# One transfer fills two exponential buffers, two are filled ahead, and the planner's thresholds are other ones

## The chip, the cores and the metric

The kernel runs on one core of a Trainium2 chip. The metric is the device time of one execution in microseconds (us). Five engines work side by side, each through its own list of instructions in a fixed order: PE multiplies matrices, ACT evaluates functions, DVE does element-wise work, POOL does small element-wise work and issues the transfers named here, and SP issues the other transfers. They wait for each other through semaphores. An engine that waits holds up everything behind it in its list.

## The reference

Four layers in a row, each added to its input: softmax attention (A), linear attention (B), then A and B again, with the same weights. There are 2048 rows of 512, 32 heads of 16; in A all heads share one key and one value.

```python
def _A_ref(x, wq, wk, wv, wo):
    q = (x @ wq).reshape(B, S, H, Dh).transpose(0, 2, 1, 3)
    k = x @ wk
    v = x @ wv
    scores = jnp.einsum("bhqd,bkd->bhqk", q, k) * (Dh ** -0.5)
    p = _softmax(scores, axis=-1)
    o = jnp.einsum("bhqk,bkd->bhqd", p, v)
    return o.transpose(0, 2, 1, 3).reshape(B, S, H * Dh) @ wo

def _B_ref(x, wqkv, wo):
    phi = lambda t: jnp.where(t > 0, t + 1, jnp.exp(t)) + 1e-6
    pq, pk = phi(q), phi(k)
    kv = jnp.einsum("bhsd,bhse->bhde", pk, v)
    num = jnp.einsum("bhqd,bhde->bhqe", pq, kv)
    den = jnp.einsum("bhqd,bhd->bhq", pq, z)[..., None] + 1e-6
    return (num / den) @ wo

x = A_x
x = x + _A_ref(_layernorm(x), ...)
x = x + _B_ref(_layernorm(x), ...)
x = x + _A_ref(_layernorm(x), ...)
x = x + _B_ref(_layernorm(x), ...)
```

## The kernel before

Nearly all the work is the exponential of the scores of the two A layers (layers 0 and 2): 2048 blocks of 128 keys x 512 (query, head) columns in each. PE makes a block of scores (L990, "QK") into a PSUM bank. Then it goes one of two ways.

- **ACT's way.** ACT takes the blocks of a set of two or three banks with one ACTIVATE with Exp (L1170), and PE multiplies the result with V (L1044, "PV").
- **DVE's way.** DVE turns a block into the int16 whose bits are a bf16 near the exponential (L1256, one TENSOR_SCALAR of 128x512). It collects four such blocks in one exponential buffer FB, a *chunk* of 128x2048. That approximation is bettered by averaging four copies whose int16 are shifted by 0, 32, 64 and 96, each with its own weight (VW, PV at L1044). So a chunk needs three shifted copies. DVE makes a shifted copy with one TENSOR_SCALAR of 128x2048 (L1304). One of the three can be made by transfers instead: POOL issues a *fill* that writes the constant row `shift_row`, which lies in DRAM, into every partition of a free FB buffer (L1328, in `prime`), and later a *shift*, a transfer that adds the chunk to the filled buffer (L1337, in `dma_shift`). Such a chunk costs DVE two shifts and not three.

FB has 12 buffers of its own. Up to five more are lent to it from tensors that lie idle (OBB, sacc, xn, wq, wo2), which is why the profile names those as outputs of L1256, L1304, L1328 and L1337 too. PT, OBB and xnT hold ACT's results in the same way.

The order on every engine is set when the program is built. `Planner` plays the program through with a duration for each operation and starts on each engine the operation with the best priority that is ready. What it started in which order is what the engines run. Which way a block goes, and when a buffer is filled, is decided there by thresholds: `BLS`, `BLT`, `BLO` and `DXB` (how much may be queued on DVE), `FBO`, `FBS` and `FBP` (how many FB buffers must stay free), `CHT`, `CHE` and `ENDL` (how near the end of the work DVE stops taking blocks), `NPRE` (how many buffers are filled ahead), `DMIN`, `DQ` and `AHEAD` (when a chunk's shift goes to a transfer), `LAG`, `STICK` and `SWITCH` (order of operations that are nearly ready). `DPF`, `DXF` and `DTAIL` are the planner's durations for transfers. The table `TUNE` changes thresholds when an A layer starts. It changes globals, so that what table 0 sets stays in force in layer 2 unless table 2 sets it again.

Layer by layer: **stream 1** is layer 0, in which the B layer's first tiles run between the blocks as x rows come out. After it comes **the transition**, in which layer 1 ends and the K and Q of layer 2 are made. `act_stream` of layer 2 starts with the first two K tiles; DVE takes blocks from the time when all 16 K tiles are made (`KGATE`), and from there on is **stream 2**. **The tail** is the end of layer 3.

Of the kernel before, what the change touches and what calls it, by code (L numbers as in the profile page):

```python
# [8 lines left out]
I16 = mybir.dt.int16  # L9
# [3 lines left out]
PE, AC, DV, PO, SP = "pe", "act", "dve", "pool", "sp"  # L13
ENGS = (PE, AC, DV, PO, SP)

P = 128
# [19 lines left out]
class Planner:  # L36
# [43 lines left out]
    def op(self, opts, reads=(), writes=(), prio=5.0, lat=0.08, dma=False, name="", join=None, mode="full", port=False, after=(), behind=(), xfer=None, trn=False):  # L80

        o = Op()
        o.opts, o.prio, o.users, o.done, o.end = opts, prio, [], False, None
        o.eng, o.fn, o.n, o.value, o.sem, o.signal, o.isdma = None, None, None, None, None, False, dma
        o.name = (name, lat)
        o.freed = False
        o.begun = None
        o.cols = 0
        o.mode = mode
        o.port = port  # L90
        o.xfer = xfer
        o.trn = trn
        deps = set()
        for k in reads:
            deps.update(self.ws(k))
        for k in list(writes) + list(after) + list(behind):
            deps.update(self.ws(k))
            deps.update(self.readers.get(k, ()))
        if join is not None:
            deps.update(join.deps)  # L100
            deps.discard(join)
        for k in writes:
            if join is not None and join in self.ws(k):
                self.writer[k] = self.ws(k) + [o]
            else:
                self.writer[k] = [o]
                self.readers[k] = []
        for k in list(reads) + list(after):
            if k not in writes:
                self.readers.setdefault(k, []).append(o)  # L110
        o.deps = deps
        o.left = 0
        chain = len(opts) == 1 and PE in opts
        for d in deps:
            if not (d.done or (chain and d.freed and d.eng == PE)):
                o.left += 1
                d.users.append(o)
        if o.left == 0:
            self._eligible(o)
        return o  # L120
# [235 lines left out]
class Seg:  # L356
# [11 lines left out]
    def take(self, js, back=False):  # L368
# [15 lines left out]
SWITCH = 0.107  # L384
# [6 lines left out]
LAG = 0.15  # L391
# [17 lines left out]
BLS = 1.4  # L409
BLO = 5.0  # L410
DXB = 2.0
BLT = 2.5
# [12 lines left out]
ENDL = 12  # L425
# [6 lines left out]
CHB = 4  # L432
FBO = 2
FBS = 4
AHEAD = 20
CHT = 19
PSH = False
STICK = 0.8
# [4 lines left out]
DMIN = 4  # L443
NPRE = 2
EVEN = True
CHE = 8
AVOID = True
PGEN = 0.95
DPF = 1.7
DXF = 3.2  # L450
DTAIL = 2.0
DQ = 4.0
FBP = 4
TUNE = {0: {"CHE": 2, "AHEAD": 10, "BLS": 1.7, "FBP": 2, "NPRE": 1, "DMIN": 3, "LAG": 0.1, "STICK": 2.0, "FBO": 1, "FBS": 4, "BLO": 7.0, "DXB": 0.8, "BLT": 3.2},
        2: {"CHE": 6, "CHT": 16, "FBS": 2, "AHEAD": 15, "BLO": 3.5, "DXB": 2.5, "FBP": 3, "DMIN": 2, "STICK": 0.8, "LAG": 0.1, "DQ": 5.0}}


def bass_interleave_layers__grouped_kv_mqa__linear_attn_block__prompt_kernel(
# [11 lines left out]
    pl = Planner(nc)  # L470
    op = pl.op
# [38 lines left out]
    NFB = 12  # L510
    FB = sb("FB", [P, NFB, CHB * 512], BF16)
# [58 lines left out]
    def guest(L, kind, i, h=None):  # L570
        return once((L, kind, i, h), home[kind, i]) if (kind, i) in home else ()
# [45 lines left out]
    fb_pool = Pool_(range(NFB))  # L617
# [92 lines left out]
    cst = nc.dram_tensor("shift_row", (1, CHB * 512), I16, kind="Internal").ap()  # L710

    def fb_keys(i):
        return [("FB", i, h) for h in range(CHB)]
# [56 lines left out]
    def until(*keys):  # L770
        for k in keys:
            yield ("ops", pl.ws(k))
# [55 lines left out]
    two = set()  # L828
# [152 lines left out]
    def run_a(L):  # L981
# [23 lines left out]
        def spend(h, o):  # L1005
            h[0] -= 1
            if o not in h[1]:
                h[1].append(o)
            if h[0] == 0:
                pl.give_after(h[2], h[3], h[1])  # L1010
# [85 lines left out]
        def act_stream():  # L1096
            if L == 0:
                globals().update(TUNE[0])
            yield ("flag", ("K", L, 0))
            globals().update(TUNE[L])  # L1100
            if L:
# [212 lines left out]
        primed = []  # L1314

        def prime():
            yield ("flag", ("K", L, T - 1))
            if L == 0:
                row = FB[0:1, NFB - 1, :].bitcast(I16)
                op({DV: (0.6, lambda e: e.memset(row, DSH * 128 // NSH))}, writes=fb_keys(NFB - 1), prio=1.0)  # L1320
                op({SP: (0.54, lambda e: e.dma_start(cst, row))}, reads=fb_keys(NFB - 1), writes=["cst"], prio=1.0, lat=2.5, dma=True)
            yield from until("cst")
            while state["si"] < len(segs) - DMIN:
                if len(primed) >= NPRE or len(fb_pool.free) <= FBP or fb_pool.wait:
                    yield ("sleep", 0.2)
                    continue
                g_ = yield ("acq", fb_pool, 9.0)
                o = op({PO: (PGEN, lambda e, g_=g_: e.dma_start(fbs[g_].bitcast(I16), cst.to_broadcast([P, CHB * 512])))}, reads=["cst"], writes=fb_keys(g_), prio=9.0,  # L1328
                       lat=0.3, dma=True, behind=guest(L, "FB", g_), xfer=(DPF, DTAIL))
                primed.append((g_, o))  # L1330
            while primed:
                g_, o = primed.pop()
                pl.give_after(fb_pool, g_, [o])

        def dma_shift(blk, f_, hold, g_, o):
            pl.stat["dma"] += 1
            o = op({PO: (PGEN, lambda e: e.dma_start(fbs[g_].bitcast(I16), fbs[f_].bitcast(I16), accum_op=ALU.add))}, reads=fb_keys(f_), writes=fb_keys(g_), prio=0.0, lat=0.3,  # L1337
                   dma=True, xfer=(DXF, DTAIL))
            spend(hold, o)
# [32 lines left out]

        pl.process(spare())
        pl.process(prime())
        for i in pairs:
            pl.process(spare_sacc(i))
# [564 lines left out]
```

## Time and profile before

| | |
|---|---|
| device time, median of 3 | 1484.33 us (1484.32 to 1484.44) |
| the profiled execution: its time, its span | 1484.35 us, 1482.5 us |
| granted TensorE clock | 1.00 |
| busy in the span: PE, DVE, ACT, POOL | 95%, 95%, 97%, 29% |
| fills (L1328) | 218 transfers of 512 KB |
| shifts by transfer (L1337) | 216 transfers of 512 KB |
| share of the 16 DMA engines taken by POOL's queue | 65.9% of the span |

The span runs from the first instruction to the last; the time has 1.85 us more, around the program. In a profile's rows "DVE FB L1256" is the DVE instruction of line 1256 that writes FB; xN is a number of instructions; "<-" names what ended the wait. An instruction's duration reaches about 0.08 to 0.2 us into the next one's, since the engines start the next before the last has drained. What an instruction costs an engine that is full is therefore the distance from its start to the next one's start, and "busy" counts such an engine as 100% even where short waits are hidden in the overlap.

### The profile page before, as it was taken

What the parts mean: (1) busy time and instruction counts of PE and PEld (TensorE: products, weight loads), DVE (VectorE), ACT (ScalarE), POOL (GpSimd) and SP (SyncE); (2) the same over time, 40 slices, a digit from 0 to 9 for tenths busy, and PEclk for the clock granted to TensorE, in tenths of its full rate; (3) what the DMA queues carried; (4) which work ended last, traced back from release to release, by engine and by line L of the source; (5) the groups of instructions that cost most, each with busy time, mean ns of one, the idle gap of its engine ahead of it and who ended that gap; (6) DMA issues with size and microseconds to landing.
All of it is one profiled execution on the core that took longest, in us unless ns stands there. A gap on an engine that the chain in (4) does not pass through costs nothing.

```text
span 1482.5 us, 40513 instructions
## 1 busy us (share of the span) xinstructions
PE 1415.0 (95%) x16387; PEld 512.6 (35%) x16387; DVE 1412.3 (95%) x2628; ACT 1441.2 (97%) x1536; POOL 424.9 (29%) x627
## 2 busy tenths in 40 slices
PE   7999999999999999999999999999999999999998
PEld 4433333333332323233644323333333333333235
DVE  7999999999999999998866899999999999999996
ACT  8999999999999999999799999999999999999996
POOL 5323333333333332300111223333323333223201
PEclk9999999999999999999999999999999999999999
DMA  4887898897888987710000458898879899879701
GB/s 116 229 205 194 185 212 188 203 215 179 195 204 197 217 192 168 187 43 2 2 2 2 104 136 200 201 211 205 212 188 226 201 211 215 203 183 216 172 1 58
DMA packets 76745, 240.14 MB, mean 162 GB/s; under 512 B 14993, under 2 KB 20113, under 8 KB 76562
## 3 DMA queue, kind: packets, MB, share of 16 engines
q0 software_dynamic: 62928, 229.14, 65.9%
q1 hardware_dynamic: 13634, 8.43, 2.0%
q8 instruction: 131, 2.15, 0.6%
q14 instruction: 52, 0.43, 0.1%
HBM read 120.62 MB, written 2.10 MB: 83 GB/s over the span
## 4 chain that ended last, share of the span: by engine, by line
PE 38%; DVE 35%; ACT 19%; issue 7%; POOL 1%; DMA 0%; ACTq 0%; DVEq 0%; POOLq 0%
PE ps L1044 15%; DVE FB L1256 14%; ACT PT L1170 12%; PE ps L990 12%; DVE FB L1304 7%; ACT xnT L1170 3%; PE ps L761 3%; PE ps L923 2%; PE ps L1089 2%; ACT OBB L1170 2%; PE ps L1410 2%; DVE wq L1256 1%; DVE xn L1256 1%; DVE sacc L1390 1%; PE ps L757 1%
## 5 line engine op out<-in xcount | busy, mean ns | idle before, releaser
L1170 ACT ACTIVATE PT<-ps 128x1024 bf16<-128x1024 f32 (+1 forms) x957 | 1004.8, 1163 | 5.4 <-PE ps L990 4.5
L1256 DVE TENSOR_SCALAR FB<-ps 128x512 int16<-128x512 f32 x852 | 558.0, 677 | 2.4 <-PE ps L990 1.6
L990 PE MATMUL ps<-QT,KM 32*128 32x512 bf16 x4096 | 534.6, 384 | 26.7 <-ACT PT L1170 14.9
L1044 PE MATMUL ps<-FB,VW 128*32 128x512 bf16 x3279 | 471.5, 385 | 10.9 <-ACT PT L1170 4.2
L1044 PE MATMUL ps<-PT,V 128*32 128x512 bf16 x2081 | 375.2, 386 | 4.0 <-DVE FB L1304 1.3
L990 PEld LDWEIGHTS ps<-QT,KM 32*128 32x128 bf16 x4096 | 134.2, 90 | 445.7 <-ACT PT L1170 216.0
L1170 ACT ACTIVATE xnT<-ps 128x1024 bf16<-128x1024 f32 (+1 forms) x240 | 261.0, 1162 | 1.0 <-PE ps L990 0.5
L1304 DVE TENSOR_SCALAR FB<-FB 128x2048 int16<-128x2048 int16 (+1 forms) x346 | 230.7, 674 | 0.0
L1337 POOL DMA_DIRECT2D FB<-FB x110 | 105.0, 955 | 334.3 <-DVE FB L1256 176.5
L1170 ACT ACTIVATE OBB<-ps 128x1024 bf16<-128x1024 f32 (+1 forms) x167 | 186.3, 1151 | 0.7 <-PE ps L990 0.6
L1044 PEld LDWEIGHTS ps<-FB,VW 128*32 128x32 bf16 x3279 | 115.8, 94 | 147.7 <-issue 81.3
L1328 POOL DMA_DIRECT2D FB<-shift_row x150 | 124.6, 831 | 45.2 <-PE ps L1044 23.9
L1089 PE MATMUL ps<-QT,V 128*32 128x512 bf16 (+6 forms) x548 | 132.7, 311 | 1.7 <-DVE sacc L1393 0.9
L1044 PEld LDWEIGHTS ps<-PT,V 128*32 128x32 bf16 x2081 | 91.3, 93 | 65.4 <-issue 36.7
L1044 PE MATMUL ps<-xnT,V 128*32 128x512 bf16 x522 | 105.1, 386 | 0.3 <-ACT PT L1170 0.3
L844 POOL TENSOR_SCALAR ve<-mv 128x1 f32<-128x1 f32 x64 | 29.5, 463 | 234.2 <-DVE mv L843 232.6
L1044 PE MATMUL ps<-OBB,V 128*32 128x512 bf16 x362 | 82.5, 387 | 1.8 <-ACT PT L1170 0.8
L761 PE MATMUL ps<-wqkv,xnT 128*32 128x512 bf16 x960 | 83.2, 383 | 0.8 <-DVE xnT L746 0.7
L1089 PEld LDWEIGHTS ps<-QT,V 128*32 128x32 bf16 x548 | 44.1, 95 | 56.8 <-issue 35.1
L1256 DVE TENSOR_SCALAR xn<-ps 128x512 int16<-128x512 f32 x80 | 52.7, 677 | 0.0
L1044 PE MATMUL ps<-xn,VW 128*32 128x512 bf16 x267 | 49.7, 385 | 1.8 <-ACT PT L1170 1.3
L1256 DVE TENSOR_SCALAR wq<-ps 128x512 int16<-128x512 f32 x75 | 49.3, 676 | 0.1
(221 smaller groups left out, 1805.8 us busy)
## 6 DMA issues: line engine op xcount, KB each, us to landing
FB<-shift_row POOLq DMA_DIRECT2D x150, 512.0 KB, 6.7
FB<-FB POOLq DMA_DIRECT2D x110, 512.0 KB, 6.0
sacc<-shift_row POOLq DMA_DIRECT2D x17, 512.0 KB, 6.9
wq<-shift_row POOLq DMA_DIRECT2D x16, 512.0 KB, 7.1
wo<-shift_row POOLq DMA_DIRECT2D x14, 512.0 KB, 7.1
xn<-shift_row POOLq DMA_DIRECT2D x14, 512.0 KB, 7.1
FB<-wq POOLq DMA_DIRECT2D x13, 512.0 KB, 6.1
wq<-FB POOLq DMA_DIRECT2D x12, 512.0 KB, 6.1
```

The costliest lines, as they stand in the source:

```text
L761: ins = e.matmul(dst[c, :], lhsT=l[:, c], rhs=r, start=(k == 0), stop=(k == len(pairs) - 1))
L844: op({PO: (0.1, lambda e: e.tensor_scalar(out=ve[:, t:t + 1], in0=mv[:, t, 1:2], scalar1=1e-5, scalar2=None, op0=ALU.add))}, reads=[("mv", ...
L923: ins = e.matmul(dst[:, g * P:(g + 1) * P], lhsT=lhs(g, k), rhs=rhs(k), start=(k == 0), stop=(k == FT - 1))
L990: return e.matmul(bank(b), lhsT=KM[r, sg.par, kt * P:(kt + 1) * P], rhs=QT[r, sg.t, :], start=True, stop=True)
L1044: ins = e.matmul(ps[32 * j:32 * j + 32, ACC * 512:(ACC + 1) * 512], lhsT=V[:, kt, :] if w is None else VW[:, kt, w, :], rhs=ap, start=(k = ...
L1089: o = op({PE: (n / 2400.0, lambda e: e.matmul(ps[32 * j:32 * j + 32, b * 512:b * 512 + n], lhsT=V0[:], rhs=QT[:, sg.t, 0:n], start=st, sto ...
L1170: ex = op({AC: (0.051 + 0.4267 * n, lambda e, n=n, s_=s_, p_=p_: e.activation(pts[p_][:, 0:n * 512], ps[:, s_ * 512:(s_ + n) * 512], ACTF. ...
L1256: o = op({DV: (0.602, lambda e: e.tensor_scalar(out=dst.bitcast(I16), in0=bank(b), scalar1=VB, scalar2=VLO, op0=ALU.add, op1=ALU.max))}, w ...
L1304: o = op({en: (du, lambda e, w=w, g_=g_: e.tensor_scalar(out=fbs[g_][:, 0:n].bitcast(I16), in0=fbs[f_][:, 0:n].bitcast(I16), scalar1=float ...
L1328: o = op({PO: (PGEN, lambda e, g_=g_: e.dma_start(fbs[g_].bitcast(I16), cst.to_broadcast([P, CHB * 512])))}, reads=["cst"], writes=fb_keys ...
L1337: o = op({PO: (PGEN, lambda e: e.dma_start(fbs[g_].bitcast(I16), fbs[f_].bitcast(I16), accum_op=ALU.add))}, reads=fb_keys(f_), writes=fb_k ...
L1410: o = op({PE: (0.12, lambda e, c=c: e.transpose(ps[:, b * 512 + c * P:b * 512 + (c + 1) * P], src[:, c * P:(c + 1) * P], identF[:]))}, rea ...
```

## The change

`prime` may now fill two buffers with one transfer. Where two of FB's own twelve buffers are free, none is filled ahead and no one waits for a buffer, POOL issues one transfer whose output is both buffers (`lo` and `hi`, in one access pattern of 128x2x2048). Else it fills one as before. The first condition of the loop counts in twos: with `NPRE` 2, a fill of either kind is begun only when no filled buffer is left over. The planner counts the double fill as 2.8 us of the transfer queue (`DPP`), where two single ones count 1.7 us each (`DPF`). Both threshold tables are replaced.

```diff
+DPP = 2.8
+TWIN = True
-TUNE = {0: {"CHE": 2, "AHEAD": 10, "BLS": 1.7, "FBP": 2, "NPRE": 1, "DMIN": 3, "LAG": 0.1, "STICK": 2.0, "FBO": 1, "FBS": 4, "BLO": 7.0, "DXB": 0.8, "BLT": 3.2},
-        2: {"CHE": 6, "CHT": 16, "FBS": 2, "AHEAD": 15, "BLO": 3.5, "DXB": 2.5, "FBP": 3, "DMIN": 2, "STICK": 0.8, "LAG": 0.1, "DQ": 5.0}}
+TUNE = {0: {'CHT': 19, 'FBO': 1, 'FBS': 3, 'BLT': 2.5, 'DMIN': 2, 'LAG': 0.0, 'SWITCH': 0.1, 'AHEAD': 20, 'BLS': 2.3, 'FBP': 3, 'DXB': 1.2, 'STICK': 2.0, 'NPRE': 2},
+        2: {'FBS': 2, 'FBP': 6, 'DQ': 6.0, 'STICK': 2.0, 'FBO': 1, 'AHEAD': 32, 'ENDL': 6, 'LAG': 0.25, 'NPRE': 2}}
...
             while state["si"] < len(segs) - DMIN:
-                if len(primed) >= NPRE or len(fb_pool.free) <= FBP or fb_pool.wait:
+                if len(primed) + (2 if TWIN else 1) > NPRE or len(fb_pool.free) <= FBP or fb_pool.wait:
                     yield ("sleep", 0.2)
                     continue
                 g_ = yield ("acq", fb_pool, 9.0)
+                two = [g for g in fb_pool.free if g < NFB]
+                if TWIN and g_ < NFB and two and len(primed) + 2 <= NPRE and len(fb_pool.free) > FBP + 1 and not fb_pool.wait:
+                    h_ = two[0]
+                    fb_pool.free.remove(h_)
+                    lo, hi = min(g_, h_), max(g_, h_)
+                    o = op({PO: (PGEN + 0.1, lambda e, lo=lo, hi=hi: e.dma_start(FB[:, lo:hi + 1:hi - lo, :].bitcast(I16), cst.unsqueeze(1).to_broadcast([P, 2, CHB * 512])))},
+                           reads=["cst"], writes=fb_keys(g_) + fb_keys(h_), prio=9.0, lat=0.3, dma=True, xfer=(DPP, DTAIL))
+                    primed.extend([(g_, o), (h_, o)])
+                    pl.stat["twin"] = pl.stat.get("twin", 0) + 1
+                    continue
```

Thresholds in force, with what table 0 leaves in layer 2:

| | layer 0 before | now | layer 2 before | now |
|---|---|---|---|---|
| BLS, BLT (DVE takes the last bank of a set) | 1.7, 3.2 | 2.3, 2.5 | 1.7, 3.2 | 2.3, 2.5 |
| BLO, DXB (DVE takes a block beside a set) | 7.0, 0.8 | 5.0, 1.2 | 3.5, 2.5 | 5.0, 1.2 |
| FBO, FBS, FBP (free buffers) | 1, 4, 2 | 1, 3, 3 | 1, 2, 3 | 1, 2, 6 |
| CHT, CHE, ENDL (end of the work) | 19, 2, 12 | 19, 8, 12 | 16, 6, 12 | 19, 8, 6 |
| NPRE, DMIN, DQ, AHEAD | 1, 3, 4, 10 | 2, 2, 4, 20 | 1, 2, 5, 15 | 2, 2, 6, 32 |
| LAG, STICK, SWITCH | 0.1, 2.0, 0.107 | 0.0, 2.0, 0.1 | 0.1, 0.8, 0.107 | 0.25, 2.0, 0.1 |

Counted over the built program, in layer 0 and layer 2:

| instructions | layer 0 before | now | layer 2 before | now |
|---|---|---|---|---|
| ACT exponentials of 2 blocks | 563 | 547 | 564 | 564 |
| ACT exponentials of 3 blocks | 110 | 123 | 127 | 127 |
| ACT exponentials of 1 block | 0 | 1 | 0 | 0 |
| DVE exponentials (1 block) | 592 | 584 | 539 | 539 |
| DVE shifts | 335 | 333 | 304 | 300 |
| single fills | 110 | 39 | 108 | 95 |
| double fills | 0 | 35 | 0 | 7 |
| shifts by transfer | 109 | 108 | 107 | 108 |

**POOL's list in the middle of stream 1** (fills from `shift_row`, shifts from a chunk). Before:

```order
L1328 DMA wo<-shift_row 128x2048
L1337 DMA wq<-xn 128x2048
L1328 DMA FB<-shift_row 128x2048
L1337 DMA wo<-FB 128x2048
L1328 DMA FB<-shift_row 128x2048
L1337 DMA FB<-FB 128x2048
L1328 DMA FB<-shift_row 128x2048
L1337 DMA FB<-xn 128x2048
```

Now (two lines more stand ahead of most of the code, and twelve ahead of what follows the new branch, so that L844 is L846, L1328 is L1340 and L1337 is L1349; L1335 is the double fill):

```order
L1335 DMA FB<-shift_row 128x2x2048
L1349 DMA wo<-FB 128x2048
L1349 DMA FB<-FB 128x2048
L1335 DMA FB<-shift_row 128x2x2048
L1349 DMA FB<-FB 128x2048 x2
L1335 DMA FB<-shift_row 128x2x2048
L1349 DMA FB<-FB 128x2048
L846 TENSOR_SCALAR ve<-mv 128x1
```

Fills and shifts no longer alternate: a fill of twice the size is followed by two shifts.

**PE's list where layer 2's first scores are made.** `xnT,wkr` makes a K tile, `xnT,wq` a Q tile, `xnT,wv` a V tile, and L990 (now L992) is the first QK of layer 2. Before:

```order
L789 MATMUL ps<-ident,xn 128x128 x4
L1780 MATMUL ps<-eps,ones 128x32
L1782 MATMUL ps<-zb,QT 128x8 x4
L1780 MATMUL ps<-eps,ones 128x32
L1782 MATMUL ps<-zb,QT 128x8 x4
L757 MATMUL ps<-xnT,wkr 128x128 x4
L757 MATMUL ps<-wv,xnT 128x16 x4
L1089 MATMUL ps<-QT,V 32x512
L939 MATMUL ps<-xnT,wq 128x128 x4
L990 MATMUL ps<-QT,KM 128x512 x3
```

Now:

```order
L791 MATMUL ps<-ident,xn 128x128 x4
L925 MATMUL ps<-xnT,wqkv 128x128 x4
L1850 MATMUL ps<-kvz,QT 128x128 x4
L925 MATMUL ps<-xnT,wqkv 128x128 x4
L759 MATMUL ps<-xnT,wkr 128x128 x4
L941 MATMUL ps<-xnT,wq 128x128 x16
L759 MATMUL ps<-wv,xnT 128x16 x4
L1869 MATMUL ps<-ident,OBB 128x128 x4
L992 MATMUL ps<-QT,KM 128x512 x5
```

Between the second K tile (the last `xnT,wkr` here) and the first QK stood a V tile, one filler and a quarter of a Q tile. Now a whole Q tile, the V tile and four transposes stand there, and the two pieces of Q and one of layer 1's outputs ahead of the K tile are new too.

**DVE's list at the end of stream 1**, from its last exponentials to the copy of the last sums (L1390, now L1402). Before:

```order
L1256 TENSOR_SCALAR FB<-ps 128x512 x2
L1304 TENSOR_SCALAR xn<-FB 128x2048
L1304 TENSOR_SCALAR FB<-FB 128x2048
L1499 TENSOR_SCALAR phE<-phE 128x512
L1304 TENSOR_SCALAR FB<-FB 128x2048
L1501 SCALAR_TENSOR_TENSOR QT<-ps,phE 128x512
L1304 TENSOR_SCALAR FB<-FB 128x2048 x2
L1390 COPY sacc<-ps 128x512
```

Now:

```order
L1258 TENSOR_SCALAR FB<-ps 128x512
L1754 TENSOR_TENSOR kvacc<-kvacc,ps 128x408
L1306 TENSOR_SCALAR sacc<-FB 128x2048
L1306 TENSOR_SCALAR FB<-FB 128x2048
L1754 TENSOR_TENSOR kvacc<-kvacc,ps 128x136
L1306 TENSOR_SCALAR FB<-FB 128x2048
L1306 TENSOR_SCALAR FB<-FB 128x512 x3
L1511 TENSOR_SCALAR phE<-phE 128x512
L1513 SCALAR_TENSOR_TENSOR QT<-ps,phE 128x512
L1402 COPY sacc<-ps 128x512
```

Behind the last exponential five full shifts stood ahead of that copy; now three full ones and three of a quarter's size do, and two kvacc additions.

## The prediction

> **What bounds the kernel now.** I read first the shares of the span, then the windows cut at the stages, then the distances between neighbouring instructions.
>
> ```profile
> span 1482.5 us, 40513 instructions
> PE 1415.0 (95%) x16387; PEld 512.6 (35%) x16387; DVE 1412.3 (95%) x2628; ACT 1441.2 (97%) x1536; POOL 424.9 (29%) x627
> ```
>
> Three engines are nearly full, so the average names none. By stage (us; busy and count of PE, PEld, DVE, ACT, POOL; clock, DMA share, GB/s), cut at the first and the last L1256 of each stream:
>
> ```profile
> 0.00:41.60 41.60, 32.33 (x378) 17.20 (x378) 32.78 (x94) 34.08 (x40) 22.20 (x75) 1.00 0.54 145
> 41.60:695.70 654.10, 627.62 (x7251) 208.69 (x7247) 650.14 (x1162) 651.76 (x680) 192.13 (x251) 1.00 0.76 179
> 695.70:828.70 133.00, 128.45 (x1585) 67.86 (x1586) 94.05 (x221) 118.85 (x131) 20.18 (x51) 1.00 0.01 4
> 828.70:1439.00 610.30, 587.78 (x6823) 196.80 (x6819) 606.86 (x1102) 606.85 (x638) 186.14 (x246) 1.00 0.80 187
> 1439.00:1482.50 43.50, 38.87 (x365) 22.04 (x357) 28.47 (x54) 29.61 (x51) 4.26 (x5) 1.00 0.15 50
> ```
>
> In both streams DVE and ACT are busy for over 99% of the stretch. Only in between does DVE stand still: 39 of 133 us. But busy spans overlap, so what an engine can carry is read from starts. ACT:
>
> ```profile
> 693.20 1.06 ACT L1170 ACTIVATE OBB<-ps 128x1024 bf16<-128x1024 f32 x1
> 694.10 1.99 ACT L1170 ACTIVATE PT<-ps 128x1024 bf16<-128x1024 f32 x2
> 695.91 0.67 ACT L1498 ACTIVATE phE<-ps 128x512 bf16<-128x512 f32 x1
> 696.38 2.88 ACT L1170 ACTIVATE PT<-ps 128x1536 bf16<-128x1536 f32 x2
> 699.04 1.57 ACT L1170 ACTIVATE OBB<-ps 128x1536 bf16<-128x1536 f32 x1
> 700.38 1.15 ACT L1170 ACTIVATE PT<-ps 128x1024 bf16<-128x1024 f32 x1
> ```
>
> An exponential of two blocks costs (695.91 - 694.10)/2 = 0.905 us, one of three (699.04 - 696.38)/2 = 1.33, a piece of 512 columns 0.47. DVE:
>
> ```profile
> 301.37 0.41 DVE L746 COPY xnT<-ps 128x512 bf16<-128x512 bf16 x1
> 301.70 0.67 DVE L1256 TENSOR_SCALAR FB<-ps 128x512 int16<-128x512 f32 x1
> 302.30 0.67 DVE L1390 COPY sacc<-ps 128x512 f32<-128x512 f32 x1
> 302.90 0.68 DVE L1304 TENSOR_SCALAR wo<-FB 128x2048 int16<-128x2048 int16 x1
> 303.50 1.27 DVE L1256 TENSOR_SCALAR FB<-ps 128x512 int16<-128x512 f32 x2
> 304.69 0.28 DVE L1499 TENSOR_SCALAR phE<-phE 128x512 bf16<-128x512 bf16 x1
> ```
>
> A block, a full shift and a 512-column piece out of f32 cost 0.60 us each, a bf16 copy 0.33. At such paces (each form at its own) the instructions between stream 1's first and last L1256 are 644 us of work on DVE (592 blocks and 330 full shifts are 553, the other 239 pieces 91) and 637 on ACT, in 654.1. In stream 2 they are 598 and 594, in 610.3. So DVE has 10 and 12 us free, ACT 17 and 16: a balanced pair, DVE a little ahead, each waiting now and then for the other through PE and the shared banks. The streams are bound by the sum of this work and by how evenly it is dealt; the ends of the streams by ACT alone, and the transition by a chain.
>
> **The change, part by part.**
>
> *Stream 1, the dealing.* DVE gets 8 blocks fewer (-8 x 0.60 = -4.8 us). In this stretch there are 6 full shifts fewer, and three of 1536 columns more, at three quarters of 0.60 (-3.6 + 1.4 = -2.2). Five more copies out of PSUM go to DVE, one sacc addition and one kvacc pair fall into other stretches: +0.7 together. DVE: 644.1 - 6.3 = 637.8. On ACT 16 exponentials of two blocks become 13 of three and one of one: -14.5 + 17.3 + 0.5 = +3.3, and seven copies and casts fewer on balance take back 2.9: +0.4 for the layer. It lies at the ends: between DVE's first and last block ACT has 1.2 less (637.2 to 636.0), and outside, where nothing covers ACT, 1.6 more. There are 69 QK blocks and not 66 before DVE's first, 13 and not 11 after its last. If DVE sets the pace: -6.3 + 1.6 = -4.7. If ACT does: +0.4. Before, DVE had less free time (10 against 17), which is nearer the first; now both have the same work, and a balanced pair waits more. I take two thirds of the way: -3.
>
> *Transition.* The chain into layer 2's first exponential:
>
> ```profile
> 725.90 0.34 PE ps L757 x8
> 726.24 0.32 PE ps L1089
> 726.55 0.33 PE ps L939 x4
> 726.88 0.35 PE ps L990 x3
> 727.26 1.45 ACT PT L1170
> 41.84 1.00 PE ps L923 x16
> 719.57 0.22 PE ps L1824 x4
> ```
>
> PE's list now has 16 `xnT,wq` matmuls and four transposes ahead of that QK, and not a filler and four of those: 1.00 + 0.22 - 0.32 - 0.33 = +0.6. ACT's copies of the K tile cover some of it. The rest of the chain has the same steps in nearly the same order, and layer 1's first outputs are interleaved with pieces that fit into its waits. Bounds -1 (that interleaving helps) and +2 (it is in the way); taken +0.5.
>
> *Stream 2.* DVE has the same 539 blocks and four shifts fewer, of which part falls at the edges: 598.4 to 597.0, -1.4. ACT has 1.6 less in all (698.3 to 696.7; the same exponentials, a few copies fewer). ACT alone: 222 and not 219 QK blocks before the last K tile is made, +1.0; 6 and not 11 blocks after DVE's last, -2.7. By DVE -3.1, by ACT -1.6; taken in the middle, -2.3.
>
> *The double fills.* They free no engine that is full.
>
> ```profile
> q0 software_dynamic: 62928, 229.14, 65.9%
> FB<-shift_row POOLq DMA_DIRECT2D x150, 512.0 KB, 6.7
> FB<-FB POOLq DMA_DIRECT2D x110, 512.0 KB, 6.0
> POOL FB L1337 <- DMA FB<-shift_row: 47.3, 17, 4.4
> PEld ps L1044 <- DMA xn<-FB: 0.2, 1, 0.2
> L1328 POOL DMA_DIRECT2D FB<-shift_row x150: 532/857/1402, 43.3 to 1386.7; - x150
> ```
>
> 42 issues of POOL at 0.86 us go, on an engine that is 29% busy: 0. The bytes are the same, 218 buffers filled and 216 shifted. A fill and a shift together take 0.659 x 1482.5 / 218 = 4.5 us of all 16 engines (about 0.5 us per double fill may go). They could pay only as more shifts by transfer, each of which spares DVE 0.60; there are 216, as before. What they cost: a shift behind a double fill waits for 512 KB more, at some 2.2 us (half of 4.5). Seventeen shifts already waited for their fill, 2.8 us in the mean and 4.4 at the longest (fourth row), and PE then waited for a transfer once, for 0.2 us. So a delay of that size is covered by what lies between landing and use. I take 0; bounds -1 and, where the cover fails, the second rival's price. The Trainium skill (DMA: Bandwidth & Descriptors, section Anatomy of one DMA) puts a transfer at about 2.0 us fixed and its bytes at 436 GB/s, so that one of twice the size would spare 2 us; by it 42 would spare 84 us of queue. The 6.7 us to landing in the row is twice its figure for 512 KB, and with the queue shared the fixed part overlaps other transfers; nothing here waits for it in any case.
>
> *Tail.* The same instructions, ACT 24.0 us in both: 0.
>
> Sum: -3 + 0.5 - 2.3 + 0 = -4.8 on the profiled execution, 1482.5 to 1477.7 us of span; with the 1.85 us around it 1479.5. That execution took 1484.35, as the median.
>
> **Rivals.**
>
> *1. ACT sets the pace; nothing is gained.* Speaking for it: ACT's work in the whole program falls by 0.5 us only, it is the busiest engine, and 6.3 us less on DVE would then be waiting time in stream 1. Against: in both streams DVE had less free time. Time: stream 1 +0.4, transition +0.5, stream 2 -1.6: -0.7, 1483.6.
>
> *2. Double fills make PE wait (slower).* PE takes its list in order. Where a shifted copy lands too late, its PV holds up the next QK, then ACT and DVE. Stream 1 has 35 of the 42, each with two shifts behind it, and the second lands after the first. For it: in stream 1 the planner now uses such chunks behind a transfer that is 2.2 us longer, and DMA engines are busy 76% of that stretch. Against: the 0.2 us above. If each of the 35 holds PE for 0.3 us: +10.5, in all +5.7, 1490. It decides from 4.8/35 = 0.14 us each.
>
> *3. POOL's longer issue holds DVE.* DVE's shifts lie beside POOL's issues:
>
> ```profile
> L1304 DVE TENSOR_SCALAR FB<-FB x346: 281/680/877, 48.1 to 1441.4; 128x2048 int16<-128x2048 int16 x168, 128x512 int16<-128x512 int16 x3, 128x1536 int16<-128x1536 int16 x2
> ```
>
> The longest is 0.2 us over the median. If every double fill cost one shift that much: 42 x 0.2 = +8.3, in all +3.5, 1488. Against: 650.1 of 654.1 us are busy with 110 single fills issued beside them, and 42 issues go. The Trainium skill (SBUF — State Buffer, section Who interferes with whom) speaks against the change here: it has POOL and a DVE instruction of this kind shut each other out for the whole instruction. The row agrees that the two touch, by 0.2 us at the most.
>
> *4. Fewer waits.* If the new order took away half of ACT's 33 us of waiting within the streams: -16, 1468. For it: nothing in the lists, only that so many thresholds move. Against: DVE's 10 and 12 us of free time leave room for no more than part of it.
>
> **How the numbers follow.** Forecast (dealing, -2 to -8): 0.54. Rival 1: 0.20. Rival 2: 0.15. Rival 3: 0.05. Rival 4: 0.06. The predicted time is the forecast's, 1479.5. Its own range, from the bounds -4.7 to +0.4, -1 to +2, -3.1 to -1.6 and -1 to 0, most of it kept, is 1476 to 1483. For 8 in 10 the range reaches up past rival 3 and down more than half way to rival 4: 1473 to 1489. About 0.2%, 3 us, is what a measurement of this kernel can tell from no change. Faster by more than that: 0.42 of the forecast's 0.54, 0.02 of rival 1, and rival 4: 0.50. Slower: most of rivals 2 and 3, 0.17, and 0.07 of the others where a list's new order costs a wait that no row shows: 0.24. Within: 0.26.
>
> **What would show it.** Right: the first-to-last stretch of L1258 (was L1256) in stream 1 is 649 to 652 us long and not 654.1, DVE stays over 99% busy there, and ACT's free time shrinks; layer 2's first exponential comes 24 to 26 us after layer 0's last; stream 2's stretch is 606 to 609. Rival 1: DVE has idle time in stream 1. Rival 2: rows in which PE L1046 waits for DMA, tens of microseconds in sum. Rival 3: the median of L1306 rises over 0.68. The forecast is wrong if the streams' stretches do not shorten, or if the transition grows by more than 3 us.

## The result, and the profile after

The changed kernel takes 1496.05 us in the median (1496.02 to 1499.02). Against the 1484.33 us before the ratio is 1.0077, 95% interval 1.006 to 1.0093: slower by 0.8%, where 0.3% faster was forecast. The profiled execution took 1499.02 us, 3 us more than the median, so that the spans below differ by more than the medians do.

The head of its page, and below it the windows cut as before at the first and the last exponential of DVE in each stream (columns as before):

```profile
span 1497.3 us, 40477 instructions
...
PE 1414.7 (94%) x16441; PEld 515.1 (34%) x16441; DVE 1416.1 (95%) x2623; ACT 1446.8 (97%) x1525; POOL 409.5 (27%) x585
```

```profile
0.00:42.70 42.70, 33.65 (x388) 17.46 (x388) 33.96 (x97) 36.06 (x41) 22.55 (x75) 1.00 0.56 144
42.70:706.20 663.50, 625.15 (x7250) 208.97 (x7254) 649.38 (x1154) 652.71 (x669) 173.58 (x214) 1.00 0.75 175
706.20:842.10 135.90, 132.72 (x1644) 70.54 (x1636) 97.21 (x228) 122.04 (x133) 20.41 (x51) 1.00 0.03 9
842.10:1456.30 614.20, 586.32 (x6846) 196.88 (x6846) 607.93 (x1097) 608.90 (x638) 188.67 (x240) 1.00 0.79 186
1456.30:1497.30 41.00, 36.91 (x333) 21.25 (x321) 27.64 (x53) 27.04 (x49) 4.26 (x5) 1.00 0.16 52
```

Set against the windows of before, stretch by stretch: +1.1 ahead of stream 1, **+9.4 in stream 1** (654.1 to 663.5), +2.9 between the streams, +3.9 in stream 2, -2.5 behind it: +14.8, the difference of the spans. In stream 1 DVE was busy for 650.1 us and now for 649.4, PE for 627.6 and now for 625.2, and ACT for 651.8 and now for 652.7. The work hardly changed and the stretch grew: this is waiting.

For what, the view of the waits says (waiting engine, tile and line, what ended the wait: sum in us, times, longest):

```profile
POOL FB L1349 <- DMA FB<-shift_row: 113.8, 34, 7.3
...
PEld ps L1046 <- DMA FB<-FB: 8.5, 11, 1.7
...
PE ps L1046 <- DMA FB<-FB: 5.5, 8, 1.4
...
PE ps L1046 <- DMA FB<-wo: 2.7, 2, 1.9
...
PE ps L1046 <- DMA FB<-sacc: 1.7, 1, 1.7
```

At this line a weight load had waited for a transfer once, for 0.2 us, and PE itself never; now it waits 9.9 us in the three rows of PE alone, 11 times (over all lines and tiles PE's waits for transfers are 14, of 11.0 us, and 11 of them, 9.2 us, lie in stream 1). Ahead of it POOL, which issues a shift only when its fill has landed, waits 34 times and 3.3 us each, up to 7.3, where it waited 17 times and 2.8 each, up to 4.4. The chain of waits says the same. Its engines' shares before, and after:

```profile
PE 38%; DVE 35%; ACT 19%; issue 7%; POOL 1%; DMA 0%; ACTq 0%; DVEq 0%; POOLq 0%
```

```profile
PE 35%; DVE 20%; ACT 16%; DMA 9%; issue 7%; POOL 1%; ACTq 0%; POOLq 0%; DVEq 0%
```

Transfers have 9% of the chain that ends last, and had none. One such place on PE's timeline:

```profile
292.75 0.39 PE L1046 MATMUL ps<-FB,VW 128*32 128x512 bf16 x1 [1.90 <-DMA FB<-wo]
...
293.74 0.39 PE L992 MATMUL ps<-QT,KM 32*128 32x512 bf16 x3
...
294.92 0.61 PE L992 MATMUL ps<-QT,KM 32*128 32x512 bf16 x3
```

PE stands 1.9 us for a shifted copy, and for 3.4 us soon after it each matmul takes 0.61 us and not 0.39. The windows of that place show why:

```profile
290.00:294.30 4.30, 2.40 (x34) 0.67 (x34) 2.47 (x5) 2.69 (x4) 1.37 (x2) 1.00 0.80 137
294.30:297.70 3.40, 3.40 (x30) 0.83 (x26) 2.89 (x5) 2.53 (x3) 0.88 (x1) 0.52 0.80 306
```

The granted clock is 0.52 in the second. So the wait costs 1.9 us, and up to half of 3.4 us on top (an estimate: it holds if PE's work there goes as its clock).

### The profile page after: what moved, and what is told of

It reads as the page before. It is cut to its first block, busy times and chain, and to the rows that moved or that the text cites. A ratio compares the mean times of both kernels' runs of the same rounds, so it can differ in the third digit from the quotient of the medians.

```text
span 1497.3 us, 40477 instructions
## 1 busy us (share of the span) xinstructions
PE 1414.7 (94%) x16441; PEld 515.1 (34%) x16441; DVE 1416.1 (95%) x2623; ACT 1446.8 (97%) x1525; POOL 409.5 (27%) x585
## 4 chain that ended last, share of the span: by engine, by line
PE 35%; DVE 20%; ACT 16%; DMA 9%; issue 7%; POOL 1%; ACTq 0%; POOLq 0%; DVEq 0%
PE ps L1046 13%; PE ps L992 11%; ACT PT L1172 10%; DVE FB L1258 7%; DVE FB L1306 4%; DMA FB<-FB 3%; PE ps L763 3%; ACT xnT L1172 3%; PE ps L1091 2%; ACT OBB L1172 1%; DMA FB<-wo 1%; PE ps L925 1%; PE ps L1422 1%; DMA FB<-shift_row 1%; ACT phE L1510 1%
## 5 line engine op out<-in xcount | busy, mean ns | idle before, releaser
L992 PE MATMUL ps<-QT,KM 32*128 32x512 bf16 x4096 | 535.1, 385 | 28.9 <-ACT PT L1172 10.8
L1258 DVE TENSOR_SCALAR FB<-ps 128x512 int16<-128x512 f32 x748 | 494.7, 683 | 5.0 <-PE ps L992 3.8
L1046 PE MATMUL ps<-FB,VW 128*32 128x512 bf16 x3212 | 456.5, 386 | 18.7 <-ACT PT L1172 6.8
L1046 PE MATMUL ps<-PT,V 128*32 128x512 bf16 x2092 | 369.0, 386 | 9.9 <-ACT PT L1172 5.7
L992 PEld LDWEIGHTS ps<-QT,KM 32*128 32x128 bf16 x4096 | 133.4, 91 | 445.6 <-ACT PT L1172 199.6
L1349 POOL DMA_DIRECT2D FB<-FB x109 | 106.6, 981 | 338.9 <-DVE FB L1258 166.0
L1306 DVE TENSOR_SCALAR FB<-FB 128x2048 int16<-128x2048 int16 (+1 forms) x297 | 198.5, 678 | 0.3
L1172 ACT ACTIVATE OBB<-ps 128x1024 bf16<-128x1024 f32 (+1 forms) x166 | 179.0, 1121 | 2.4 <-PE ps L992 2.4
L1091 PE MATMUL ps<-QT,V 128*32 128x512 bf16 (+6 forms) x619 | 141.1, 307 | 2.0 <-DVE sacc L1405 0.7
L846 POOL TENSOR_SCALAR ve<-mv 128x1 f32<-128x1 f32 x64 | 28.6, 449 | 221.4 <-DVE mv L845 221.3
L1340 POOL DMA_DIRECT2D FB<-shift_row x89 | 75.0, 892 | 17.5 <-PE ps L1046 9.7
L1258 DVE TENSOR_SCALAR wo<-ps 128x512 int16<-128x512 f32 x92 | 61.6, 684 | 3.6 <-PE ps L992 3.1
L1046 PE MATMUL ps<-xn,VW 128*32 128x512 bf16 x279 | 59.9, 388 | 1.6 <-DVE sacc L1402 1.1
L1046 PE MATMUL ps<-wo,VW 128*32 128x512 bf16 x254 | 53.7, 385 | 2.0 <-DVE sacc L1402 0.8
```

The lines of the kernel that those rows point to most:

```text
L846: op({PO: (0.1, lambda e: e.tensor_scalar(out=ve[:, t:t + 1], in0=mv[:, t, 1:2], scalar1=1e-5, scalar2=None, op0=ALU.add))}, reads=[("mv", ...
L992: return e.matmul(bank(b), lhsT=KM[r, sg.par, kt * P:(kt + 1) * P], rhs=QT[r, sg.t, :], start=True, stop=True)
L1046: ins = e.matmul(ps[32 * j:32 * j + 32, ACC * 512:(ACC + 1) * 512], lhsT=V[:, kt, :] if w is None else VW[:, kt, w, :], rhs=ap, start=(k = ...
L1091: o = op({PE: (n / 2400.0, lambda e: e.matmul(ps[32 * j:32 * j + 32, b * 512:b * 512 + n], lhsT=V0[:], rhs=QT[:, sg.t, 0:n], start=st, sto ...
L1172: ex = op({AC: (0.051 + 0.4267 * n, lambda e, n=n, s_=s_, p_=p_: e.activation(pts[p_][:, 0:n * 512], ps[:, s_ * 512:(s_ + n) * 512], ACTF. ...
L1258: o = op({DV: (0.602, lambda e: e.tensor_scalar(out=dst.bitcast(I16), in0=bank(b), scalar1=VB, scalar2=VLO, op0=ALU.add, op1=ALU.max))}, w ...
```

## The experiments

The theory (D): the double fill makes its shifts late. The first rival (T): the new thresholds let PE use copies so early that any transfer is late, double or not. The second (N): with no transfer late the new lists still wait more, so the dealing is not worth its 4.8 us. Ratios are against the kernel before on the same chip, with 95% intervals.

### Splitting the double fill in place

```diff
-e.dma_start(FB[:, lo:hi + 1:hi - lo, :].bitcast(I16), cst.unsqueeze(1).to_broadcast([P, 2, CHB * 512]))
+e.dma_start(fbs[g_].bitcast(I16), cst.to_broadcast([P, CHB * 512]))
+e.dma_start(fbs[h_].bitcast(I16), cst.to_broadcast([P, CHB * 512]))
```

> Each double fill is issued as two single transfers in the same place of POOL's list, with the order of every other instruction on every engine exactly as in the change. If the size of the one transfer is what is slow (a single fill adds 1.5 us behind a shift, a double 4.7): queue time falls by about 1.7 us for each of 42, the late landings vanish, 1481 to 1488 us. If two fills in a row cost the queue that much however they are issued: 1493 to 1498 us, the same waits. Rivals T and B also expect 1493 to 1498 us.

Measured: 1489.91 us (1487.13 to 1497.22) against 1485.75, ratio 1.0024 [1.0007, 1.0042]. The lists of PE, ACT, DVE and SP and the bytes are those of the change; only each double fill is two singles. About two thirds of the loss are gone (0.77% to 0.24%, 7.9 us); the interval of each ratio is some 2.5 us to either side. The expectation had 1481 to 1488 us if the one large transfer is what is late, and 1493 to 1498 for its rivals: the time lies between, nearer the first. PE's waits for transfers fall from 11.0 us in 14 to 2.2 in 6. The largest waits are now:

```profile
POOL FB L1351 <- DMA FB<-shift_row: 83.3, 28, 5.0
...
PEld ps L1046 <- DMA FB<-FB: 2.2, 6, 1.0
```

The two streams of its profile (columns as before) are 654.8 and 612.6 us long, against 663.5 and 614.2 in the change:

```profile
42.70:697.50 654.80, 623.35 (x7250) 209.09 (x7254) 648.25 (x1153) 651.41 (x669) 191.99 (x249) 1.00 0.77 177
833.50:1446.10 612.60, 585.06 (x6846) 196.78 (x6846) 607.32 (x1097) 608.59 (x638) 190.01 (x246) 1.00 0.80 187
```

POOL's timeline at the same place, first of the change, then with the fills split (start, duration, line, transfer, idle time before and what ended it):

```profile
268.38 1.39 POOL L1335 DMA_DIRECT2D FB<-shift_row  x1
271.70 1.03 POOL L1349 DMA_DIRECT2D FB<-FB  x1 [1.93 <-DVE FB L1258]
278.72 0.85 POOL L1349 DMA_DIRECT2D FB<-FB  x1 [6.00 <-DMA FB<-shift_row]
279.27 1.05 POOL L1335 DMA_DIRECT2D FB<-shift_row  x1
279.98 1.24 POOL L1349 DMA_DIRECT2D FB<-wo  x1
```

```profile
267.45 1.28 POOL L1335 DMA_DIRECT2D FB<-shift_row  x1
267.99 1.35 POOL L1337 DMA_DIRECT2D FB<-shift_row  x1
271.35 1.19 POOL L1351 DMA_DIRECT2D FB<-FB  x1 [2.01 <-DVE FB L1258]
276.19 0.88 POOL L1351 DMA_DIRECT2D FB<-FB  x1 [3.66 <-issue]
276.95 0.68 POOL L1335 DMA_DIRECT2D FB<-shift_row  x1
277.49 0.70 POOL L1337 DMA_DIRECT2D FB<-shift_row  x1
279.54 1.02 POOL L1351 DMA_DIRECT2D FB<-wo  x1 [1.35 <-DVE wo L1258]
```

In the first, the third row is a shift that stands 6.00 us until the fill of the first row has landed; in the split kernel its like goes out 2.5 us earlier, at 276.19 (0.9 us of this was its lead already at the fill). What the trace's records of packets add (the 4 KB packets of the queue in order of their start, dealt to the transfers in order of issue; us):

```
                      packets first..last   landed
the change   double       272.49..276.86    278.43
split        first        271.11..273.23    274.95
             second       272.98..274.96    276.37
the change   shift FB<-wo issued 279.98     292.71  (PE waited 1.90 for it)
split        shift FB<-wo issued 279.54     288.71  (no wait)
```

The data of a double takes about as long as that of two singles (4.4 us here, 3.85 for the two; over the 42 places the medians are 4.0 and 4.0). But the whole double has one semaphore: its first buffer may be used at 278.43, where in the split kernel the first single has landed at 274.95. Counted from the first packet, to take out the lead, a double lands after 5.6 us in the median of the 42, the first of the two singles after 3.3 and the second after 4.9. So the first buffer comes 2.3 us later, and the second 0.7 us later as well; what makes the second late no run here shows. POOL waits that much longer, everything behind it in POOL's list goes out later, and the next double goes ahead of the shift that PE then waits for.

### The size by itself

> Edit: the whole computation is left out; POOL alone issues, three times over, 8 single fills, then 4 double fills, then 6 pairs of a single fill and a shift, then 4 groups of a double fill and two shifts, each group awaited before the next. Theory D as the traces of the two kernels gave it: a double lands 4 to 5 us behind the transfer ahead of it where the queue is full, a single 1.5 us, also here where no engine computes. If the double's price comes from what runs beside it (the engines, the other queues), it is here under 3.0 us, two singles in one. Either way a shift lands some 2.5 to 2.9 us behind a fill.

POOL's timeline; L484 is a single fill, L487 a double, L490 a shift, and each group begins when the one before has landed:

```profile
111.17 4.25 POOL L484 DMA_DIRECT2D FB<-shift_row  x8 [27.02 <-DMA FB<-CH]
128.18 2.80 POOL L487 DMA_DIRECT2D FB<-shift_row  x4 [12.76 <-DMA FB<-shift_row]
145.10 0.54 POOL L484 DMA_DIRECT2D FB<-shift_row  x1 [14.12 <-DMA FB<-shift_row]
...
174.31 0.72 POOL L487 DMA_DIRECT2D FB<-shift_row  x1 [20.54 <-DMA FB<-CH]
...
212.39 1.11 POOL L484 DMA_DIRECT2D FB<-shift_row  x2 [28.05 <-DMA FB<-CH]
```

Eight singles take 128.18 - 111.17 = 17.0 us, four doubles 145.10 - 128.18 = 16.9 (second of the three rounds; in the third 16.1 and 17.1). Six pairs of a single and a shift take 29.2, 4.9 each; four doubles with eight shifts 38.1, 4.8 per buffer. So on a queue that is full and has nothing beside it a double costs what two singles cost. From landing to landing a double was 3.1 us behind a shift (median of 9), a single 1.3 (15), the next single 1.8: neither the 4 to 5 us of the theory nor the under 3.0 of its rival. Theory D is right in what it says of lateness, and wrong in that a double would be slow in itself, with nothing beside it. In the full kernels it does land later than two singles: 4.7 us behind a shift (median of 37), where in the split kernel the second single lands 3.9 us behind the same shift.

The Trainium skill (DMA: Bandwidth & Descriptors, section Anatomy of one DMA) gives a transfer a fixed 2.0 us, mostly the wait for the receipt of its last byte, after which alone the semaphore counts. The second half agrees with 278.43 above. The 2.0 us are not spared by merging on a full queue: 16.9 against 17.0 us for the same bytes.

### Telling the planner, and fewer or more doubles

The change with `DPP = 4.7` in place of 2.8; the change with `TWIN = False`; and the old tables with doubles (`NPRE` 2).

> The change with one number other: the planner counts a double fill as 4.7 us of the transfer queue and not 2.8, which is its measured landing-to-landing time behind a shift. The plan then has 36 double fills and 206 shifts by transfer (216 in the change), 637 DVE shifts (633). Theory D: PE waits for transfers fall from 14 to at most 3; the time is 1480 to 1488 us. Rival T and rival B: 1493 to 1498 us, since the tables are the same.

> The new tables, but no double fill: two buffers are filled ahead by single transfers (226 single fills, 222 shifts by transfer, DVE 627 shifts and 1124 blocks). Theory D (a double fill holds the transfer queue 4.7 us where the planner counts 2.8, so shifts queued behind it land late and PE waits for them): no or nearly no PE wait for a transfer (under 2 us in all), 1478 to 1486 us. Rival T (the new tables let PE use shifted copies so early that any transfer is late, whatever filled the buffer): PE waits for transfers of 10 us or more, 1492 to 1498 us. Rival B (the dealing of blocks between ACT and DVE in the new tables is what costs): no such waits and still 1490 us or more.

> The old tables (but NPRE 2 in place of 1, without which no double fill can happen) with the double fill: 65 double and 89 single fills, 216 shifts by transfer, 636 DVE shifts, 1132 DVE blocks. Theory D: with 65 double fills there are more late landings than with 42, PE waits for transfers of 15 us or more, 1492 to 1510 us. Rivals T and B: the old tables keep 1482 to 1487 us.

Measured: told 1489.70 (1488.78 to 1495.61), ratio 1.0024 [1.0009, 1.0039]; singles only 1490.37 (1486.36 to 1495.62), 1.0024 [1.0009, 1.0039]; old tables with doubles 1519.47 (1517.58 to 1528.72), **1.0236** [1.0203, 1.0269]. Three ways of taking away the late doubles, splitting, telling and leaving out, end at the same 0.24%; PE waits 0.3 us for transfers in the told kernel and 0.9 with singles only. But all three lie 2 to 4 us above the ends of what theory D expected (1488, 1488 and 1486 us). The singles fit what their expectation says of rival B, few such waits and still 1490 us: this is theory N by another name, and it holds for the part that stays. With 65 doubles under the old tables the loss is three times that of the change with its 42:

```profile
PEld ps L1046 <- DMA FB<-FB: 18.7, 20, 1.9
...
PE ps L1046 <- DMA FB<-FB: 12.3, 16, 1.8
...
PEld ps L1046 <- DMA FB<-xn: 6.8, 6, 2.7
```

Rival T falls: with the old thresholds the doubles do more harm, not less. Those tables with two singles filled ahead were the control:

> Edit: the kernel before's tables with two buffers filled ahead (NPRE 2), singles only. Theory D (only the size of the double transfer hurts): 1482 to 1487, PE's waits for transfers under 3 us in sum, against 1519 with double fills and the same tables. If filling ahead itself takes buffers from DVE: 1488 to 1495, with free time of DVE in stream 1 over 15 us and not 10.5, and few waits for transfers.

1494.06 us (1489.39 to 1498.19), ratio 1.0049 [1.0033, 1.0065]. This was a miss for both: few waits for transfers (POOL 6.7 us in 3, and 2.5 on PE and its weight loads), no more free time of DVE in stream 1 than before, and still slower, by 0.5%. Its windows show where: the streams take 655.1 and 610.7 us (654.1 and 610.3 before), but 142.6 us lie between them and not 133.0, where there are hardly any transfers (DMA share 0.02). A stretch of 6.8 us at half the clock there explains 3.4 us at the most, and work has moved there too (1655 matmuls and not 1585). What is sure is the difference: doubles cost these tables 1.0236 against 1.0049.

### The change's lists with transfers out of the way

```diff
-e.dma_start(fbs[g_].bitcast(I16), fbs[f_].bitcast(I16), accum_op=ALU.add)
+e.dma_start(fbs[g_][:, 0:512].bitcast(I16), fbs[f_][:, 0:512].bitcast(I16), accum_op=ALU.add)
```

with the fills cut in the same way, in the changed kernel and in the one before.

> Edit: the changed kernel with every list of instructions as it is, but after a buffer's first fill in a layer, fills and shifts move only the first 512 of 2048 columns: three quarters of these transfers are left out, so no landing should be late. Theory D+B (the new dealing is worth its 4.8 us, and everything lost is lost to late landings): 1478 to 1482 us, stream 1 at 649 to 652 us, stream 2 at 606 to 609, PE's waits for transfers under 1 us in sum. Theory N (the new lists themselves wait more between PE, ACT and DVE, whatever the transfers do): 1485 to 1489, stream 1 at 653 to 655, stream 2 at 610 to 612, with PE's waits for transfers as small.

> Edit: the kernel before with the same cut: after a buffer's first fill in a layer, fills and shifts move 512 of 2048 columns, three quarters of them left out. The control of the run above. If the transfers cost the kernel before nothing (PE waited 0.2 us for them), 1483 to 1485 us, stretches of 653 to 654 and 609 to 610 us. If the transfers slow other engines by sharing the memory with them, 1475 to 1480, and the run above has to be set against this one and not against the kernel before.

Measured: the change so cut 1488.84 (1486.44 to 1491.34), ratio 1.0015 [1.0005, 1.0025]; the kernel before so cut 1485.94, ratio 1.0003 [0.9993, 1.0012]. Its transfers cost the kernel before nothing that this interval shows. In both, PE waited for no fill or shift. The windows, first of the change so cut, then of its control:

```profile
43.60:697.20 653.60, 623.25 (x7252) 208.93 (x7254) 647.74 (x1152) 651.24 (x670) 175.54 (x214) 1.00 0.35 58
697.20:833.10 135.90, 132.72 (x1644) 70.56 (x1636) 97.22 (x228) 122.03 (x133) 20.48 (x51) 1.00 0.03 9
833.10:1445.00 611.90, 584.82 (x6846) 196.76 (x6846) 607.12 (x1097) 608.10 (x638) 189.94 (x240) 1.00 0.37 59
1445.00:1486.00 41.00, 36.94 (x333) 21.26 (x321) 27.68 (x54) 27.07 (x49) 4.27 (x5) 1.00 0.16 52
```

```profile
41.20:695.40 654.20, 627.79 (x7251) 208.74 (x7247) 650.12 (x1162) 651.85 (x680) 193.21 (x251) 1.00 0.33 57
695.40:829.30 133.90, 129.55 (x1585) 68.02 (x1586) 94.07 (x220) 118.88 (x131) 20.18 (x51) 0.99 0.01 3
829.30:1439.50 610.20, 587.68 (x6824) 196.68 (x6827) 606.41 (x1102) 606.76 (x638) 190.98 (x246) 1.00 0.35 60
1439.50:1483.10 43.60, 38.94 (x365) 22.09 (x365) 28.55 (x54) 29.70 (x52) 4.27 (x5) 1.00 0.15 49
```

Stream 1, 663.5 us in the change, is 653.6: the late transfers were worth 9.9 us there and 2.3 in stream 2. By the ratios it is (1.0077 - 1.0015) x 1484 = 9.2 us in the whole. But nothing is gained either. Against the control stream 1 is 0.6 us shorter, stream 2 1.7 longer. Rival N holds for what is left, 0.15%, some 2 us. The two spans differ by 2.9 us: besides these two, stream 1 begins 2.4 us later (43.6 against 41.2; the change so cut has 3.4 us at half the clock there), 2.0 us more lie between the streams, and 2.6 less behind them.

### Which half of the thresholds

New thresholds in layer 0 alone, then in layer 2 alone, both with singles; the first was profiled once more, since its first profile had two long stretches of half the clock.

> Edit: the new thresholds in layer 0 alone, the old ones in layer 2, singles only. With all new thresholds and singles only it was 1490.4 (ratio 1.0024). If what is left of the loss comes from stream 2's new thresholds: 1482 to 1486, stream 2 back at 609 to 610 us. If it comes from stream 1's: 1488 to 1491, stream 1 at 656 to 658. Theory N without a place: in between.

> Edit: none against the run with the new thresholds in layer 0 alone; a second profile, since the first had two stretches of half clock that cost some 11 us and hide where the loss lies. If the loss is in stream 1 itself: its stretch at 655 to 657 us. If it lies ahead of stream 1: DVE's first exponential at 43 us or later and not at 41.6, stream 1 at 653 to 654.

> Edit: the old thresholds in layer 0, the new ones in layer 2, singles only; the mirror of the run that had the new ones in layer 0 alone (there stream 2 came to 606.9 us, stream 1 to 653.9). If the new thresholds of layer 2 are what makes stream 2 wait longer: stream 2 at 611 to 613 us, stream 1 at 653 to 654, 1486 to 1488 without clock dips. If it is not the thresholds but how any new list falls: stream 2 at 607 to 610, 1482 to 1485.

Measured: layer 0 alone 1489.05 (1487.19 to 1497.78), ratio 1.0026 [1.0013, 1.0040]; in the first profile stream 1 took 653.9 us. In the second (one execution, 1488.49 us) it took 656.0 us where it takes 654.1 in the kernel before, and DVE's first exponential came at 42.7 us and not at 41.6. These two places make 3.0 of the 4.2 us by which this span is longer; of the rest 4.4 us more lie between the streams (137.4 and not 133.0), and stream 2 gives 2.8 back. Layer 2 alone **1483.61 (1482.95 to 1484.92), ratio 0.9983 [0.9974, 0.9993]**: faster than the kernel before, by 2.5 us by the ratio, 1.9 between the medians. Its expectation missed: stream 2 is longer, but it begins earlier:

```profile
0.00:42.20 42.20, 33.87 (x378) 17.43 (x378) 32.76 (x93) 34.12 (x40) 22.25 (x75) 0.96 0.55 149
42.20:696.30 654.10, 627.76 (x7251) 208.69 (x7251) 650.09 (x1161) 651.76 (x680) 191.70 (x251) 1.00 0.76 179
696.30:825.30 129.00, 125.67 (x1545) 64.99 (x1546) 93.07 (x222) 115.92 (x125) 21.68 (x53) 1.00 0.02 6
825.30:1440.80 615.50, 591.30 (x6930) 200.66 (x6922) 610.22 (x1104) 612.09 (x645) 192.21 (x250) 1.00 0.81 191
1440.80:1482.90 42.10, 37.24 (x329) 21.24 (x326) 27.10 (x51) 28.03 (x50) 4.26 (x5) 1.00 0.15 51
```

129.0 and not 133.0 us lie between the streams, 5.2 more in stream 2, 1.4 less behind it. A stretch cut at events of the list moves with the list; only the sum over neighbours tells a gain. Here the two profiled spans do not show it (1482.9 against 1482.5, with the clock at 0.96 ahead of stream 1, first row); the interval over 11 runs and 14 of the kernel before does, narrowly. By it this version beats the kernel before, by 0.07% at the least.

## Why the prediction was wrong, point by point

- **The double fills, "I take 0": this is the step that failed.** It said that a shift waits 2.2 us more, that seventeen shifts had waited 2.8 us in the mean with PE waiting 0.2, and "so a delay of that size is covered by what lies between landing and use". The term was +9.2 us. The split kernel puts 7.9 us on issuing two fills as one transfer with one semaphore; the remaining 1.3 is within the intervals. The row used for the cover (POOL's waits) tells how late shifts already were, not how much later they might be. That stands in the same trace: between the landing of a shift and the matmul that waits for it lay in stream 1 of the kernel before 0.04 us at the least and 1.8 in the median (109 shifts; the k-th shift of a semaphore against the k-th matmul that waits for this semaphore). Two thirds of them had no cover for 2.2 us. In stream 2 it was hardly more, 0.1 at the least and 2.2 in the median; but only 7 of the 42 doubles lie there, and its stretch lost 2.3 us to late transfers where stream 1 lost 9.9. With the old tables, where doubles are common in both, stream 2 takes 636.5 us and not 610.3.
- **The delay itself, 2.2 us**, came true: the first buffer of a double lands 2.3 us later than that of two singles, by its partner's transfer. POOL, which waits in order, passes that on to the transfers behind it: its longest wait went from 4.4 to 7.3 us. The 0.5 us per double that might have gone from the queue did not: 16.9 against 17.0 us in the run of transfers alone.
- **Rival 2** was the right mechanism, at a chance of 0.15, with a price of another kind: not 35 waits of 0.3 us in stream 1, but 11 of 0.8, and the longest was followed by the half clock as well. It gave 1490; 1496 was measured.
- **Rival 3** is out: DVE's shifts have a median of 0.685 us and at most 0.828 (0.680 and 0.877 before). That POOL had a part in the longest of before, as the prediction read its row, no view shows:

```profile
L1306 DVE TENSOR_SCALAR FB<-FB x297: 286/685/828, 46.3 to 1458.6; 128x2048 int16<-128x2048 int16 x144, 128x512 int16<-128x512 int16 x3, 128x1536 int16<-128x1536 int16 x2
```

- **The dealing in stream 1, -3**, failed in its choice, not in its counts. DVE's work did fall, from 650.1 to 647.7 busy us in the two cut kernels, and by some 5 us if each form is priced at its median distance from start to start (an estimate); the stretch fell by 0.6. "Two thirds of the way" to DVE setting the pace should have been nearly none: it came out near rival 1, whose stretch of stream 1 hardly moves. Ahead of stream 1 the change has +1.1, of the +1.6 that was forecast for both ends.
- **The transition, +0.5 (bounds -1 to +2)**: layer 2's first exponential came 28.3 us after layer 0's last (712.07 to 740.35, from start to start) and not 26.9, +1.4, inside the bounds. The whole stretch between the streams grew by more, 2.9 us (2.0 in the cut pair), where the forecast had +0.5 here and +1.0 for ACT's blocks ahead of the last K tile; it holds 1644 matmuls and not 1585, so that a part is work that moved in. The sign named for it, 24 to 26 us, was a slip: it did not follow from 26.9 + 0.5.
- **Stream 2, -2.3**: +1.7 in the stretch and -2.6 behind it in the cut pair. The end of the layer (6 and not 11 blocks, forecast -2.7) came true to 0.1 us; the gain by DVE's work did not.
- What stays open: why less work on PE, ACT and DVE at once (the windows above) does not shorten stream 1. No run here names what they wait for. Why some lists take longer between the streams (142.6 us with the old tables and two singles) and others do not (132.2 in the told kernel) is open as well, and with it what costs those old tables 0.5%.

## What to carry to other kernels

Two transfers merged into one share one semaphore: the first half can't be used before the second has landed, and on the full queue here no time was saved. Before taking such a delay as covered, measure the cover itself, the distance from each landing to its first use, and read its smallest values; that no one waits now says only that it isn't negative. And where the work of balanced engines is cut by less than 1%, the stretch need not follow: count it as zero until a run shows it.

## What the hardware showed that was not expected

Behind a wait of PE well under 3 us its clock can be half. In the change it is 1.9 us of waiting, then 0.52 of the clock for 3.4 us (windows above). In the old tables with doubles there are six such stretches, five of them behind a wait for a transfer of 1.2 us or more, for instance:

```profile
1223.20:1225.60 2.40, 1.76 (x16) 0.66 (x16) 0.68 (x2) 0.68 (x1) 0.07 (x1) 0.78 1.13 188
1225.60:1231.10 5.50, 5.50 (x39) 1.12 (x42) 3.74 (x8) 3.49 (x5) 1.88 (x2) 0.50 1.00 212
```

PE had waited 1.78 us for a transfer up to 1223.8. In the two kernels, of the five waits for a transfer of 1.75 us or more all were followed by a half clock within 1.8 us, of the other twelve between 1.0 and 1.75 us one. The Trainium skill (TensorE: Matmul & The Clock Gate, section Why this matters for your kernels) warns of gaps over some 3 us; here 1.78 to 2.84 us were enough each time. So what follows such a wait can cost more than the wait: behind the 1.78 us the clock is half for 6.8 us, which by estimate is up to 3.4 us. But a long wait is not the only way to it. The second half clock of the change, from 1270.6 to 1274.0, has no wait over 0.91 us in the 9 us ahead of it, and the kernel before with its transfers cut has one from 752.6 to 756.1 behind waits of 0.33 us at the most. What decides there, these runs do not settle.
